# Products with kv in tiles of 32, and a second half laid out anew, in a Hedgehog attention and Mish layer

## The chip, the cores and the metric

The kernel runs on one core of a Trainium2 chip. The metric is the device time of one execution in microseconds; the median of three runs before the change is 182.94 us.

## The reference

```python
def _A_ref(x, wqkv, w_phi, wo):              # H = 32 heads of Dh = 16, S = 2048, D = 512
    q, k, v = qkv[0], qkv[1], qkv[2]         # of x @ wqkv, by heads
    pq = jnp.einsum("bhsd,hdf->bhsf", q, w_phi)
    pk = jnp.einsum("bhsd,hdf->bhsf", k, w_phi)
    phi_q = concatenate([softmax(pq), softmax(-pq)], axis=-1)
    phi_k = concatenate([softmax(pk), softmax(-pk)], axis=-1)
    kv = jnp.einsum("bhsf,bhsd->bhfd", phi_k, v)
    z  = jnp.einsum("bhsf->bhf", phi_k)
    num = jnp.einsum("bhqf,bhfd->bhqd", phi_q, kv)
    den = jnp.einsum("bhqf,bhf->bhq", phi_q, z)[..., None] + 1e-6
    return (num / den by heads side by side) @ wo

def _B_ref(x, w1, b1, w2):                   # F = 1792
    h = x @ w1 + b1
    return (h * tanh(softplus(h))) @ w2

xn = layernorm(x)
return x + _A_ref(xn, wqkv, w_phi, wo) + _B_ref(xn, w1, b1, w2)
```

All inputs and the output are bf16; x is 2048 x 512.

## The kernel before

The 2048 rows are 16 tiles of 128, in four groups of four. Everything is issued in an order written out by hand; each engine works through its own instructions in that order, so what stands early in the text stands early on every engine.

**First half** (the loop over `s` from 0 to 3, lines 505 to 542). Per group: `ln_stats` and `ln_apply` normalise two groups ahead; `value` projects v into `vext`; `logits` projects the keys (folded with w_phi) into `p_sb`; `extremes` (VectorE) subtracts each head's maximum and minimum, over all four tiles at once; `exponentials` (ScalarE) takes the exponentials in place; `normalise` (VectorE) divides by the sums; `accumulate` adds the group's phi_k times v to `pkv` in PSUM. `hidden(n)` computes n units of the first dense layer (each four products of 512 columns) with Mish on ScalarE; they fill TensorE between the steps of the attention.

**Second half** (from line 545). `mask_kv` copies the diagonal blocks of the accumulated kv to `kvm`. Passes 4 to 7 are the queries: `logits`, `extremes`, `exponentials`, which here also issues (through `turn`) DMA transposes of the exponentials into `qT`. `attend(h, i)` multiplies one tile's `qT` with `kvm` into the PSUM tile `pnd`, and ScalarE copies numerators and denominators out of it (lines 350 to 357). `combine(h)` (VectorE) weighs the two planes of two tiles and adds them, and issues a DMA transpose into `ob`. `second_layer(t)` is 14 products of 512 columns into a bank `po`; `project_out(h)` adds four products with `wo` to each of the banks of tiles 2h and 2h+1, and `residual` (VectorE, line 431) adds x and issues the store on SyncE. A bank `po` is held from second_layer(t) to the residual of tile t.

The lines that the prediction uses: in `accumulate` (L285) a product takes 64 columns of the exponentials against 65 of v and ones; two of them, for `r` = 0 and 1, lie side by side in the array by `tile_position=(0, 64 * r)`. In `attend` (L341) a product takes all 128 rows of `qT` against 144 columns of `kvm`, in which the blocks of other heads are zero.

PSUM has eight banks: five in the pool `ps` (all projections, hidden units and `po`), three in `ps2` (`pwide`, then `pkv`, then `pnd`, one at a time).

Of the kernel before, what the change touches and what calls it, by code (L numbers as in the profile page):

```python
# [1 line left out]

# [15 lines left out]
def kernel(  # L18
# [13 lines left out]
    P = 128  # L32
# [26 lines left out]
    ps = ctx.enter_context(tc.tile_pool(name="ps", bufs=5, space=bass.MemoryType.PSUM))  # L59
    ps2 = ctx.enter_context(tc.tile_pool(name="ps2", bufs=1, space=bass.MemoryType.PSUM))  # L60
# [4 lines left out]
    kvm = persist.tile([P, 2, 4, 144], BF16, name="kvm")  # L65
# [14 lines left out]
    KVmask = consts.tile([P, 136], FP32, name="KVmask")  # L80
    vext = [vpool.tile([P, TPG, 4, 2, 68], BF16, name=f"vext{i}") for i in range(2)]
# [11 lines left out]
    def fold(wT, dst, dve):  # L93

        for kt in range(KT):
            pf = ps.tile([P, 512], FP32, name="pfold", tag="mm")
# [40 lines left out]
    def ln_turn_pe(t, xn, i, copy):  # L137
        ptr = ps.tile([P, 512], BF16, name="ptr", tag="mm")
# [12 lines left out]
    def project(w, t, pp=None):  # L151

        if pp is None:
            pp = ps.tile([P, 512], FP32, name="pproj", tag="mm")[:]
# [7 lines left out]
    def value(t, copy):  # L162
        pv = project(wv, t)
        copy(
            vext[(t // TPG) % 2][:, t % TPG, :, :, 0:64].rearrange("p j r c -> p (j r) c"),
            pv.rearrange("p (j c) -> p j c", j=8),
# [4 lines left out]
    def hidden(n):  # L171

        for _ in range(n):
            g, f = next(units)
            ph = ps.tile([P, 512], FP32, name="ph", tag="mm")
# [15 lines left out]
    def logits(s, i, copy):  # L191
        if i == 0:
            p_of[s] = smx.tile([P, TPG, 512], BF16, name="p_sb", bufs=1)
# [3 lines left out]
    def extremes(s, between=None):  # L197

        e = epool.tile([P, TPG, 2, 512], BF16, name="e")
        e_of[s] = e  # L200
        pv = p_of.pop(s)[:].rearrange("p t (c e) -> p (t c) e", e=16)
        for pl, op in enumerate((ALU.max, ALU.min)):
            if pl == 1 and between is not None:
                between()
            src = pv
            for half in (8, 4, 2):
                m = smx.tile([P, 128, half], BF16, name=f"m{half}", bufs=1)
                nc.vector.tensor_tensor(  # L208
                    out=m[:], in0=src[:, :, 0:half], in1=src[:, :, half : 2 * half], op=op
                )  # L210
                src = m[:]

            m = smx.tile([P, 128, 1, 2], BF16, name="m1", bufs=1)
            nc.vector.tensor_tensor(out=m[:, :, 0, :], in0=src, in1=src[:, :, ::-1], op=op)
            mb = m[:].rearrange("p (t c) u o -> p t c u o", t=TPG).to_broadcast(
                [P, TPG, 32, 8, 2]
            )
            p5 = pv.rearrange("p (t c) (e o) -> p t c e o", t=TPG, o=2)
            nc.vector.tensor_tensor(  # L219
                out=e[:, :, pl, :].rearrange("p t (c e o) -> p t c e o", e=8, o=2),  # L220
                in0=p5 if pl == 0 else mb,
                in1=mb if pl == 0 else p5,
                op=ALU.subtract,
            )
# [39 lines left out]
    def blocks(kv, pl, j, width):  # L264

        bank, at = (pl, j) if j < 3 else (2, pl)
        return kv[:, bank, at * 144 : at * 144 + width]

    def by_parts(kv, c0, c1):

        v = kv[:, :, 0:432].rearrange("p b (k c) -> p b k c", c=144)
        return v[:, 0:2, :, c0:c1], v[:, 2, 0:2, c0:c1]

    kv_of = {}

    def accumulate(g):
        if g == 0:
            kv_of[0] = ps2.tile([P, 3, 512], FP32, name="pkv", tag="kv")
        e = e_of.pop(g)
        for j in range(4):  # L280
            for pl in range(2):
                for i in range(TPG):
                    for r in range(2):
                        c = j * P + 64 * r
                        nc.tensor.matmul(  # L285
                            blocks(kv_of[0], pl, j, 65)[64 * r : 64 * r + 64],
                            lhsT=e[:, i, pl, c : c + 64],
                            rhs=vext[g % 2][:, i, j, r, 0:65],
                            start=(g == 0 and i == 0 and (j == 0 or (j == 3 and pl == 0))),
                            stop=(g == NG - 1 and i == TPG - 1),  # L290
                            skip_group_check=True,
                            tile_position=(0, 64 * r),
                        )

    def mask_kv():
        for r in range(2):
            rows, c = slice(64 * r, 64 * r + 64), slice(64 * r, 64 * r + 64)
            a, b = by_parts(kv_of[0], 0, 64)
            nc.vector.tensor_tensor(
                out=kvm[rows, :, 0:3, c], in0=a[rows],  # L300
                in1=KVmask[rows, None, None, c].to_broadcast([64, 2, 3, 64]), op=ALU.mult,
            )
            nc.vector.tensor_tensor(
                out=kvm[rows, :, 3, c], in0=b[rows],
                in1=KVmask[rows, None, c].to_broadcast([64, 2, 64]), op=ALU.mult,
            )
        a, b = by_parts(kv_of[0], 64, 65)
        for pl in range(2):
            nc.vector.scalar_tensor_tensor(
# [311 lines left out]
```

## Time and profile before

| | |
|---|---|
| median of 3 runs | 182.94 us (182.93 to 183.0) |
| the profiled execution | 182.85 us |
| its span on the core | 181.1 us (1.75 us lie around it) |
| TensorE clock granted | 0.999 |
| TensorE busy, VectorE busy, ScalarE busy | 173.9, 146.3, 126.2 us |

Busy times are unions of an engine's instructions. A matmul's duration in the records holds its way through the array, so the records of neighbours overlap; what a product costs is the distance from its start to the next one's start. PE stands for TensorE's products and PEld for its weight loads, DVE for VectorE, ACT for ScalarE, POOL for GpSimdE, SP for SyncE, and a q behind a name for the engine's sequencer. In rows of the chain of work stand start, duration, engine, tile and line; in rows of a timeline also the shapes and in brackets the idle time before, and what ended it. In rows of groups stand the count, the busy time, the mean of one in ns, and the idle time before. In rows of waits stand the total in us, the count and the longest.

### The profile page before, as it was taken

The numbers are of one execution on the slowest core, as the hardware profiler recorded it, in microseconds if no ns is written. First come the engines' busy times: TensorE is split into PE (matmuls) and PEld (weight loads), VectorE is DVE, ScalarE is ACT, GpSimd is POOL, SyncE is SP. The second block draws the span as 40 slices with busy tenths as digits, with TensorE's granted clock in tenths as the row PEclk, the third lists the DMA queues.
The fourth block names the chain that finished last, engine by engine and source line by source line (L and its number), as shares of the span: only waits on it lengthen the run. The fifth ranks groups of instructions, "written<-read, shape, count | busy, mean of one in ns | idle before, by whom it ended". The sixth has DMA issues, their size and how long they took to land.

```text
span 181.1 us, 3005 instructions
## 1 busy us (share of the span) xinstructions
PE 173.9 (96%) x1152; PEld 87.0 (48%) x1167; DVE 146.3 (81%) x254; ACT 126.2 (70%) x194; POOL 26.8 (15%) x34
## 2 busy tenths in 40 slices
PE   6899999999999999998999999999999999999992
PEld 2454344454444545543454545455554545455561
DVE  1989979997999989988999895399917997637963
ACT  2367999999998899969986989472942567235200
POOL 4404069400797000000000000000000000000000
PEclk9999999999999999999999999999999999999999
DMA  6998896300023900000000791953089302990533
GB/s 146 294 390 279 158 346 179 70 1 5 0 58 63 114 0 0 4 0 0 4 0 0 148 87 23 188 136 63 0 177 207 79 5 47 200 192 26 86 91 116
DMA packets 44394, 18.04 MB, mean 100 GB/s; under 512 B 36828, under 2 KB 43868, under 8 KB 44380
## 3 DMA queue, kind: packets, MB, share of 16 engines
q1 hardware_dynamic: 43408, 17.50, 42.8%
q10 hardware_dynamic: 972, 0.35, 0.7%
q8 instruction: 9, 0.15, 0.4%
q14 instruction: 5, 0.04, 0.1%
HBM read 6.84 MB, written 2.10 MB: 49 GB/s over the span
## 4 chain that ended last, share of the span: by engine, by line
PE 50%; DVE 38%; ACT 4%; DMA 4%; issue 2%; POOL 0%; DVEq 0%; POOLq 0%
PE po L414 20%; PE ph L177 8%; DVE s L247 7%; PE po L423 7%; DVE m L208 7%; DVE e L219 5%; PE pproj L156 5%; DVE e L260 4%; ACT e L229 4%; PE pnd L341 3%; DVE r L255 3%; PE warm L463 3%; DVE stats L116 3%; DMA xnT<-xn 2%; DMA ob<-ob 2%
## 5 line engine op out<-in xcount | busy, mean ns | idle before, releaser
L414 PE MATMUL po<-w_sb,acts 128*128 128x512 bf16 (+1 forms) x232 | 50.3, 366 | 0.3
L177 PE MATMUL ph<-xnT,w_sb 128*128 128x512 bf16 x224 | 49.5, 379 | 0.1
L184 ACT ACTIVATE acts<-ph,b1f 128x512 bf16<-128x512 f32 x56 | 35.1, 703 | 2.5 <-PE ph L177 2.3
L177 PEld LDWEIGHTS <-w_sb 128*128 128x128 bf16 x224 | 21.9, 98 | 26.6 <-issue 0.5
L229 ACT ACTIVATE e<-e 128x2048 bf16<-128x2048 bf16 x16 | 29.8, 1903 | 6.9 <-DVE e L219 6.9
L414 PEld LDWEIGHTS <-acts 128*128 128x128 bf16 x238 | 22.8, 98 | 22.0
L156 PEld LDWEIGHTS <-xnT 128*128 128x128 bf16 x192 | 18.2, 98 | 23.0 <-DMA xnT<-xn 1.1
L247 DVE TENSOR_REDUCE s<-e 128x128 f32<-128x2048 bf16 x8 | 18.2, 2277 | 2.6 <-ACT e L229 2.6
L195 ACT CAST p_sb<-pproj 128x512 bf16<-128x512 f32 x25 | 13.7, 587 | 9.4 <-PE pproj L156 9.4
L431 DVE TENSOR_TENSOR x_sb<-po,x_sb 128x512 bf16<-128x512 f32 (+1 forms) x17 | 10.6, 654 | 11.4 <-PE po L423 11.4
L128 POOL TENSOR_SCALAR xn<-x_sb,mv,rstd 128x512 bf16<-128x512 bf16 x8 | 16.7, 2101 | 0.2
L156 PE MATMUL pproj<-wv,xnT 128*128 128x512 bf16 x61 | 15.0, 379 | 0.9 <-ACT p_sb L195 0.8
L423 PE MATMUL po<-wqk,ob 128*128 128x512 bf16 (+1 forms) x66 | 14.7, 366 | 0.3 <-DMA ob<-ob 0.2
L156 PE MATMUL pproj<-wqk,xnT 128*128 128x512 bf16 x62 | 14.4, 379 | 0.1
L350 ACT CAST wkp<-pnd 128x768 bf16<-128x768 f32 x8 | 6.4, 799 | 11.2 <-PE pnd L341 7.3
L116 DVE BATCH_NORM_STATS2 stats<-x_sb 128x6 f32<-128x512 bf16 x16 | 10.0, 679 | 3.8 <-DMA x_sb<-in_A_x_dram 3.8
L208 DVE TENSOR_TENSOR m<-m 128x512 bf16<-128x512 bf16 (+1 forms) x32 | 11.6, 363 | 1.1
L156 PE MATMUL pproj<-wkp,xnT 128*128 128x512 bf16 x50 | 11.8, 379 | 0.1
L208 DVE TENSOR_TENSOR m<-p_sb 128x1024 bf16<-128x1024 bf16 x16 | 11.0, 684 | 0.7 <-ACT p_sb L195 0.7
L341 PEld LDWEIGHTS <-qT 128*128 128x128 bf16 x128 | 9.1, 98 | 3.9 <-issue 0.3
L341 PE MATMUL pnd<-kvm,qT 128*128 128x144 bf16 x128 | 10.6, 226 | 0.0
L350 ACT CAST wv<-pnd 128x768 bf16<-128x768 f32 x8 | 6.3, 792 | 5.9 <-PE pnd L341 3.7
(68 smaller groups left out, 174.8 us busy)
## 6 DMA issues: line engine op xcount, KB each, us to landing
w_sb<-in_B_w_dram SPq DMA_DIRECT2D x2, 1792.0 KB, 9.1
out_dram<-x_sb SPq DMA_DIRECT2D x15, 128.0 KB, 1.8
x_sb<-in_A_x_dram SPq DMA_DIRECT2D x1, 1024.0 KB, 11.8
x_sb<-in_A_x_dram SPq DMA_DIRECT2D x1, 512.0 KB, 4.1
wv<-in_A_wqkv_dram SPq DMA_DIRECT2D x1, 512.0 KB, 4.9
wqk<-in_A_wo_dram SPq DMA_DIRECT2D x1, 512.0 KB
x_sb<-in_A_x_dram SPq DMA_DIRECT2D x1, 256.0 KB, 2.9
x_sb<-in_A_x_dram ACTq DMA_DIRECT2D x1, 256.0 KB, 3.5
```

What stands on the lines that cost most here:

```text
L116: nc.vector.bn_stats(stats[:, i, :], x_sb[:, t0 + i, :])
L128: engine.tensor_scalar(out=xn[:, at + i, :], in0=x_sb[:, t0 + i, :], scalar1=mv[:, i, 0:1], scalar2=rstd[:, i : i + 1], op0=ALU.subtract, ...
L156: nc.tensor.matmul(pp, lhsT=xnT[:, t, kt, :], rhs=w[:, kt, :], start=(kt == 0), stop=(kt == KT - 1),)
L177: nc.tensor.matmul(ph[:], lhsT=w1_sb[:, kt, f * P : (f + 1) * P], rhs=xnT[:, g * TPG : (g + 1) * TPG, kt, :], start=(kt == 0), stop=(kt == ...
L184: nc.scalar.activation(acts[:, f, g * 512 : (g + 1) * 512], ph[:], ACT.Mish, bias=b1f[:, f : f + 1])
L195: copy(p_of[s][:, i, :], pp)
L208: nc.vector.tensor_tensor(out=m[:], in0=src[:, :, 0:half], in1=src[:, :, half : 2 * half], op=op)
L229: nc.scalar.activation(v, v, ACT.Exp)
L247: nc.vector.reduce_sum(t[:], v.rearrange("p t l (c e) -> p (t l c) e", e=16), axis=AX.X)
L341: nc.tensor.matmul(blocks(pnd, pl, j, 144), lhsT=qT_of[h][:, i, pl * 4 + j, :], rhs=kvm[:, pl, j, :], start=True, stop=True,)
L414: nc.tensor.matmul(po[:, c], lhsT=acts[:, f, t * P : (t + 1) * P], rhs=w2_sb[:, f, c], start=(f == 0), stop=False,)
L423: nc.tensor.matmul(po[:, c], lhsT=oT_of[h][:, t % 2 * 4 + j, :], rhs=wo_sb[:, j, c], start=False, stop=(j == 3),)
```

## The change

- `accumulate` uses four tiles of 32 columns side by side, each against 33 columns of v and ones: 128 products per group in place of 64. All of `pkv` lies in one bank, and `vext` has groups of 36 columns in place of 68.
- `attend` uses four tiles of 32 rows, each against 36 columns of `kvm`, into four banks: 32 products in place of 8. ScalarE copies `pnd` out with two instructions in place of four.
- `mask_kv` has two instructions in place of seven, `masks` twelve small copies in place of three and a memset.
- PSUM pools are opened and closed along the way: up to the end of the unit loop of `s` = 0, five banks for projections as before; then seven (`ps`, `px`, `pz`) beside one for `pkv`; in the second half four (`ps`) beside four for `pnd`; in the end one more for the second half of the last tile.
- `extremes` of passes 5 to 7 work in halves of two tiles, `combine` of 0, 2, 3, 4 and 7 tile by tile, and their order around `project_out` is written out anew; the loop over `h` is gone. Two products of second_layer(1) come before attend(0, 0). Pass 7 has its own tile `p_last` for the logits.
- `residual` no longer issues the store; `store()` issues those that wait, later in the order.

```diff
     def accumulate(g, pk):
...
-                    for r in range(2):
-                        c = j * P + 64 * r
+                    for r in range(4):
+                        c = j * P + 32 * r
                         nc.tensor.matmul(
-                            blocks(kv_of[0], pl, j, 65)[64 * r : 64 * r + 64],
-                            lhsT=e[:, i, pl, c : c + 64],
-                            rhs=vext[g % 2][:, i, j, r, 0:65],
+                            kv_of[0][32 * r : 32 * r + 32, pl, j, :],
+                            lhsT=e[:, i, pl, c : c + 32],
+                            rhs=vext[g % 2][:, i, j, r, 0:33],
...
-                            tile_position=(0, 64 * r),
+                            tile_position=(0, 32 * r),
...
-        pnd = ps2.tile([P, 3, 512], FP32, name="pnd", tag="kv")
+        pnd = later[0].tile([P, 4, 512], FP32, name="pnd", tag="nd")
         for pl in range(2):
             for j in range(4):
-                nc.tensor.matmul(
-                    blocks(pnd, pl, j, 144),
-                    lhsT=qT_of[h][:, i, pl * 4 + j, :],
-                    rhs=kvm[:, pl, j, :],
+                for r in range(4):
+                    at, rows = (pl * 4 + j) * 36, slice(32 * r, 32 * r + 32)
+                    nc.tensor.matmul(
+                        pnd[:, r, at : at + 36],
+                        lhsT=qT_of[h][rows, i, pl * 4 + j, :],
+                        rhs=kvm[rows, pl, j, :],
...
+                        tile_position=(32 * r, 0),
...
+        a = pnd[:, :, 0:288].rearrange("p r (l j c) -> p l j r c", l=2, j=4)
+        to = nm[:, i, :, :].rearrange("p l (j r c) -> p l j r c", j=4, r=4)
+        nc.scalar.copy(to, a[:, :, :, :, 0:32])
+        nc.scalar.copy(ds[:, i], a[:, :, :, :, 32:36])
...
     def residual(t, po, c, queue):
         y = x_sb[:, t, c]
         nc.vector.tensor_tensor(out=y, in0=po[:, c], in1=y, op=ALU.add)
-        queue.dma_start(o_v[:, t, c], y)
+        waiting.append((queue, o_v[:, t, c], y))
...
+            hidden(6)
+            turns[0] = cycle([pz, ps, ps, pz, ps, px, ps])
+        hidden((5, 14, 8, 10)[s])
         extremes(s + 1)
...
     second_layer(0)
     hidden(2)
+    second_layer(1, 0, 2)
     attend(0, 0)
-    second_layer(1, 0, 8)
+    second_layer(1, 2, 12)
     attend(0, 1)
-    extremes(5)
-    second_layer(1, 8)
-    combine(0)
-    exponentials(5)
+    extremes(5, halves=low)
+    second_layer(1, 12)
+    combine(0, first)
+    combine(0, last)
+    extremes(5, halves=high)
+    exponentials(5, (0,))
     second_layer(2)
     attend(1, 0)
     second_layer(3)
     attend(1, 1)
...
+    project_out(0)
+    combine(1)
+    store()
+    for i in range(TPG):
+        logits(6, i, act)
+    attend(2, 0)
+    exponentials(5, (1,))
+    second_layer(4)
+    extremes(6, halves=low)
+    attend(2, 1)
+    exponentials(6, (0,))
+    second_layer(5)
+    combine(2, first)
+    project_out(1)
+    combine(2, last)
+    store()
+    attend(3, 0)
+    second_layer(6)
+    combine(3, first)
+    attend(3, 1)
+    second_layer(7)
+    combine(3, last)
+    project_out(2)
+    store()
+    for i in range(TPG):
+        logits(7, i, act)
+    extremes(6, halves=high)
+    attend(4, 0)
+    exponentials(6, (1,))
+    second_layer(8)
+    extremes(7, halves=low)
+    attend(4, 1)
+    exponentials(7, (0,))
+    second_layer(9)
+    combine(4, first)
+    project_out(3)
+    combine(4, last)
+    store()
+    attend(5, 0)
+    second_layer(10)
+    extremes(7, halves=high)
+    attend(5, 1)
+    exponentials(7, (1,))
+    second_layer(11)
+    project_out(4)
+    combine(5)
+    store()
+    attend(6, 0)
+    second_layer(12)
+    attend(6, 1)
+    second_layer(13)
+    combine(6)
+    attend(7, 0)
+    project_out(5)
+    combine(7, first)
+    attend(7, 1)
+    combine(7, last)
+    store()
+    after.close()
+    later.append(ctx.enter_context(tc.tile_pool(name="pe", bufs=1, space=PSUM)))
+    second_layer(14)
+    second_layer(15)
+    project_out(6)
+    store()
+    project_out(7)
+    store()
```

More of the change, by code (lines that the diff above doesn't have):

```diff
@@ L79 @@
     block = consts.tile([P, 8, 16], BF16, name="block")
-    KVmask = consts.tile([P, 136], FP32, name="KVmask")
-    vext = [vpool.tile([P, TPG, 4, 2, 68], BF16, name=f"vext{i}") for i in range(2)]
+    KVmask = consts.tile([P, 34], FP32, name="KVmask")
+    vext = [vpool.tile([P, TPG, 4, 4, 36], BF16, name=f"vext{i}") for i in range(2)]
     ctx.enter_context(tc.manual_schedule())
@@ L95, in fold @@
         for kt in range(KT):
[L96 removed]
+            pf = bank("pfold")
             for j in range(4):
@@ L153, in project @@
         if pp is None:
-            pp = ps.tile([P, 512], FP32, name="pproj", tag="mm")[:]
+            pp = bank("pproj")[:]
         for kt in range(KT):
@@ L410, in second_layer @@
         if f0 == 0:
-            po_of[t] = [ps.tile([P, 512], FP32, name="po", tag="mm") for _ in halves(t)]
+            po_of[t] = [
+                bank("po", FP32, later[1] if c.stop == 512 and c.start else None)
+                for c in halves(t)
+            ]
         for po, c in zip(po_of[t], halves(t)):
```

232 lines of the change are left out of this document (106 added, 126 removed).

## The prediction

> **What bounds the kernel now.** I read the page first, then the chain of work that ended last, then the timelines of TensorE, ScalarE, VectorE and SyncE in the second half.
>
> ```profile
> PE 173.9 (96%) x1152; PEld 87.0 (48%) x1167; DVE 146.3 (81%) x254; ACT 126.2 (70%) x194; POOL 26.8 (15%) x34
> ...
> PE 50%; DVE 38%; ACT 4%; DMA 4%; issue 2%; POOL 0%; DVEq 0%; POOLq 0%
> ```
>
> TensorE is busy for 96% of the span, yet only half of the chain is TensorE; over a third is VectorE. Both are nearly full, and where the chain changes hands tells which one a saving must come from:
>
> ```profile
> 42.72 0.69 DVE vext L164
> ...
> 111.53 3.18 DMA ob<-ob
> ...
> 114.76 1.90 PE po L423 x8
> ...
> 123.63 0.50 PE pnd L341 x8
> 124.13 3.02 PE po L414 x14
> 127.15 1.73 PE po L423 x8
> ```
>
> From 42.72 to 111.53 the chain runs mainly through VectorE (normalise, extremes, combine(0)), then through one DMA transpose into project_out(0) at 114.76, and from there through TensorE alone. Three prices come from these rows: an attend is 0.50 us on TensorE, a second_layer 3.02, a project_out 1.73 (0.865 per tile). Three waits matter:
>
> ```profile
> 41.86 0.69 DVE L164 CAST vext<-pproj 128x512 bf16<-128x512 f32 x1 [1.38 <-PE pproj L156]
> ...
> PE pproj L156 <- ACT p_sb L195: 0.8, 1, 0.8
> ...
> PE po L423 <- DMA ob<-ob: 0.2, 1, 0.2
> ```
>
> At 41.86 VectorE waits for TensorE, so what accumulate(0) saves moves the VectorE chain. After that VectorE sets the pace up to combine(0): time that accumulate(1) to (3) save, or the 0.8 us wait for a bank that the seven banks may remove, lets TensorE reach attend(0,0) sooner, but not its transposed input. The 0.2 is the wait at 114.76.
>
> **The products with kv.** Today one accumulate, with its neighbours:
>
> ```profile
> 38.69 1.03 PE L177 MATMUL ph<-xnT,w_sb 128*128 128x512 bf16 x4
> 39.65 1.20 PE L285 MATMUL pkv<-vext,e 128*64 128x65 bf16 x64
> 40.79 0.39 PE L156 MATMUL pproj<-wv,xnT 128*128 128x512 bf16 x1
> L285 PE MATMUL pkv<-vext,e 128*64 128x65 bf16 x256 | 4.8, 196 | 0.0
> ```
>
> A product of 512 columns takes 3.02/14 = 0.216 us, so the last of the four before starts at 38.69 + 3 x 0.216 = 39.34 and streams until 39.56. The 64 products then begin within 1.20 - 0.196 = 1.0 us, and the next full one starts at 40.79. The block costs 1.23: 32 pairs at 31.5 ns, and 0.23 for going into the tiled form and out of it again.
>
> The price of columns: 0.50/8 = 62.5 ns for 144 and 216 for 512 give 0.417 ns per column and 2.4 fixed, so 29.5 ns for 65. The measured pair, 31.5, is just above that: the two tiles of a pair run side by side. Four tiles would take, per set of four, between 17.4 ns (36 columns, all four side by side, the same for 33 within 1.2 ns) and 31.5 (what two tiles take now, with as many columns in all). I take the middle, 24.5. [...]
>
> An accumulate becomes 32 sets: 0.23 + 32 x 0.0245 = 1.01, saving 0.22. An attend becomes 8 sets, and now it too changes the tiling, which it didn't before: 0.23 + 8 x 0.0245 = 0.43, saving only 0.07 of 0.50 each, 16 x 0.075 = 1.2 us. Most of what smaller products give goes back into 32 more changes of form. With 17.4 and 31.5 an attend is 0.37 or 0.48. The trace has no row tiles: if changing to them cost nothing, an attend would be 0.14 (third rival), and if loads don't overlap it would be above 0.5 (first rival).
>
> **Around attend(0,0).**
>
> ```profile
> 103.18 0.66 PE L341 MATMUL pnd<-kvm,qT 128*128 128x144 bf16 x8
> ...
> 99.50 5.38 SPq L238 DMA_TRANSPOSE qT<-e  x4
> ...
> DMA to landing us min/median/max: 3.2/3.3/4.8
> ...
> 97.45 0.54 DVE L299 TENSOR_TENSOR kvm<-pkv,KVmask 64x384 bf16<-64x384 f32 x1
> ...
> 99.25 1.88 DVE L195 CAST p_sb<-pproj 128x512 bf16<-128x512 f32 x3
> ```
>
> Its input, the first transpose of qT, lands at 99.50 + 3.3 = 102.8 and TensorE comes at 103.18. After: the VectorE chain is 0.2 earlier (accumulate(0)), so the input is there at 102.6. TensorE has two more products of second_layer(1) ahead of it (0.43), and is earlier by 4 x 0.22 + 0.8 = 1.7: it would come at 101.9 and waits until 102.6. So of the first half's 1.7 us there remain 0.58, and the 0.43 already done: 1.0 us. On VectorE mask_kv falls from seven steps in 1.8 us (97.45 to 99.25) to two, about 0.5 by the nearest rows, and the first half of extremes(5) no longer waits for the fourth cast. That makes room for combine(0) in halves; with it the transposes of combine(0) come before TensorE asks for them, and the wait ahead of 114.76 (0.2 us) goes.
>
> **ScalarE.** One eviction:
>
> ```profile
> 104.22 0.80 ACT L350 CAST wkp<-pnd 128x768 bf16<-128x768 f32 x1
> ...
> 105.29 0.23 ACT L357 COPY ds<-pnd 128x32 f32<-128x32 f32 x1
> ```
>
> Four copies take 1.30 us from 104.22 to 105.52. Two copies of 1024 and 128 elements, at the slope of these rows, take some 1.16. ScalarE has room in the second half, so I put it at nothing; if runs of 32 elements out of four banks cost 0.4 us more, the next attend waits 0.4 once, at (0,1), since elsewhere 3.02 us of second_layer lie between.
>
> **VectorE, and four banks in place of five.**
>
> ```profile
> 101.78 0.69 DVE L208 TENSOR_TENSOR m<-p_sb 128x1024 bf16<-128x1024 bf16 x1 [0.65 <-ACT p_sb L195]
> ...
> 107.74 0.28 DVE L373 TENSOR_TENSOR u<-ds 128x128 f32<-128x128 f32 x1
> ...
> 115.83 0.69 DVE L431 TENSOR_TENSOR x_sb<-po,x_sb 128x512 bf16<-128x512 f32 x1 [4.33 <-PE po L423]
> ...
> 117.30 0.28 DVE L373 TENSOR_TENSOR u<-ds 128x128 f32<-128x128 f32 x1
> ...
> 120.99 0.68 DVE L208 TENSOR_TENSOR m<-p_sb 128x1024 bf16<-128x1024 bf16 x1
> ...
> 167.74 0.22 DVE L373 TENSOR_TENSOR u<-ds 128x64 f32<-128x64 f32 x1
> ...
> 170.25 1.28 DVE L431 TENSOR_TENSOR x_sb<-po,x_sb 128x512 bf16<-128x512 f32 x2
> L208 DVE TENSOR_TENSOR m<-m 128x512 bf16<-128x512 bf16 x16 | 6.8, 428 | 0.6
> L208 DVE TENSOR_TENSOR m<-m 128x256 bf16<-128x256 bf16 x16 | 4.8, 299 | 0.5
> L391 DVE TENSOR_TENSOR wv<-wv,f 128x1024 bf16<-128x1024 bf16 x2 | 1.4, 692 | 0.1
> ```
>
> A whole extremes takes 107.74 - 101.78 = 5.96. A half, for each of max and min, is 0.43 (512 elements), 0.30 (256), 0.235 (128, by the slope of those two), about 0.23 for the last fold, 0.69 for the subtraction, with 0.03 between: 1.9, so 3.8 a half and 1.6 more per pass, 4.9 for three passes. A half combine takes 170.25 - 167.74 = 2.5. A whole one took about 3.7 (117.30 to 120.99) and gets two more small steps, 4.05 (0.22 each in place of half of a 0.28). Five combines in halves in place of one, and three whole ones: some 6 us more. So VectorE gets about 11 us more work in the second half, where it has waits like the 4.33 us above. Two places have no cover for it:
>
> Before project_out(2), VectorE does residual(3), which ends 0.9 us after project_out(1) (0.21 for the result to arrive, 0.69), then three half combines, 7.5: residual(4) ends 8.4 + 0.7 = 9.1 us after project_out(1). TensorE does two attends, two second_layers and project_out(2) in 0.86 + 6.04 + 1.73 = 8.6 and then wants a bank for logits(7): of four, two hold tiles 6 and 7, the others wait for residuals 4 and 5. New wait: 0.4.
>
> Before project_out(5), VectorE does residual(9) (0.9 after project_out(4)), combine(5) 4.05, and the transposes land 3.2 later: 8.1. TensorE has three attends and two second_layers, 7.3. New wait: 0.8.
>
> SyncE issues 13 transposes of ob in place of 9, at 5.38/4 = 1.35 us each at most, and the stores behind them; its waits are long, and a store that goes later delays nobody but at the end, where the order of the last residuals and stores is as before. Nothing for that.
>
> **The sum**, against the profiled execution (span 181.1, 1.75 us around it, 182.85; the median is 182.94): -1.0 (to attend(0,0)) - 1.2 (attends) - 0.2 (wait at 114.76) + 0.4 + 0.8 = -1.2. With 17.4 ns per set -1.9, with 31.5 -0.7. I forecast 181.6, with 180.9 to 182.2 as this case's own range.
>
> **The rivals.** *Loads and products don't come closer than now.* 64 loads and products took 1.0 us, 15.7 ns for each. If a row tile's load and product keep that pace, an attend is 0.23 + 32 x 0.0157 = 0.73, slower by 0.23: 16 x 0.23 = +3.7, the two new waits vanish behind longer attends, -1.0 - 0.2 + 3.7 = +2.5, 185.3. It decides above 0.0105 us per load and product. For it:
>
> ```profile
> L341 PEld LDWEIGHTS <-qT 128*128 128x128 bf16 x128 | 9.1, 98 | 3.9 <-issue 0.3
> L482 PEld LDWEIGHTS <-b1b 14*128 14x128 bf16 x1 | 0.1, 90 | 0.1
> ```
>
> A load of 14 rows takes 90 ns where 128 rows take 98, and there are four times as many. Against it: the pitch inside accumulate is that of the columns, so nothing shows a limit on loads. [...] If accumulates keep that pace too (128 x 0.0157 + 0.23 = 2.2, +1.0 each, four of them, less the bank wait), it is about 189. Chance 0.24, of which 0.06 for the latter.
>
> *VectorE becomes the bound.* If each half piece costs 0.25 more than worked out, the wait at logits(7) grows by three pieces, 0.75, a like one of 0.6 opens at logits(6), where combine(1) follows two residuals that follow a half extremes, and 0.2 and 0.4 come ahead of project_out(5) and the last one: +2.0, 183.6. It decides at about 0.15 a piece. For it: VectorE is 81% busy and gets 11 us more. Against: the half combine is measured. Chance 0.13.
>
> *Changing to row tiles costs nothing.* Attends of 0.14 save 5.8, but VectorE's lateness gives some 3.9 back in all (1.2 worked out above, the rest at the same places by the same 0.3 us per attend): -1.0 - 5.8 - 0.2 + 3.9 = -3.1, 179.8. Against it, the 0.23 of accumulate. Chance 0.13.
>
> **The numbers.** The forecast has 0.50. A measurement of this kernel can tell about 0.2% (0.37 us) from no change. Faster: 0.13 and nearly all of the forecast, 0.44: 0.57. Same: 0.06. Slower: 0.24 + 0.13 = 0.37. The range 180.0 to 185.5 leaves out half of the third rival, the accumulate part of the first and a little of its upper side: under 0.2.
>
> **What would show it.** In the changed profile: 8 sets of four in an attend within 0.37 to 0.48 us from the end of one 512-column product to the next; an accumulate near 1.0; TensorE waiting some 0.7 us for qT ahead of attend(0,0), 0.4 for VectorE ahead of logits(7), 0.8 for ob ahead of project_out(5). An attend above 0.55, or waits of TensorE for residuals of 1 us and more, would make the forecast wrong.

## The result and the profile after

The changed kernel takes 182.28 us (median of 6 runs, 181.76 to 182.54) against 182.94 (6 runs, 182.78 to 183.24): a ratio of 0.9957 with a 95% interval of 0.9939 to 0.9976, 0.66 us or 0.4% less. Faster was forecast, by 1.3 us; the time is inside the range, and 0.1 above the forecast case's own one. The profiled execution is the fastest of the six: 181.76 us, span 179.8, clock 0.997.

From the page of the changed kernel: busy times with counts, the instruction fetches of TensorE (queue q8), and the shares of the chain. Lines have moved: attend's products stand at L337, accumulate's at L290, second_layer at L415, project_out at L424, the residual at L432.

```profile
PE 170.8 (95%) x1785; PEld 81.8 (46%) x1807; DVE 154.0 (86%) x313; ACT 123.9 (69%) x162; POOL 29.6 (16%) x42
q8 instruction: 14, 0.23, 0.5%
DVE 47%; PE 33%; ACT 8%; DMA 8%; issue 2%; DVEq 0%; ACTq 0%; SPq 0%
```

TensorE's loads and products rose by about half, from 2319 to 3592, and with them the fetches, from 9 to 14; before, that row read:

```profile
q8 instruction: 9, 0.15, 0.4%
```

TensorE's timeline after, at the places the prediction named:

```profile
39.41 1.20 PE L290 MATMUL pkv<-vext,e 128*32 128x33 bf16 x128
40.54 1.90 PE L168 MATMUL pproj<-wv,xnT 128*128 128x512 bf16 x7
...
102.44 0.37 PE L337 MATMUL pnd<-kvm,qT 32*128 32x36 bf16 x32 [0.15 <-DMA qT<-e]
...
112.40 0.37 PE L337 MATMUL pnd<-kvm,qT 32*128 32x36 bf16 x32
112.70 1.04 PE L424 MATMUL po<-wqk,ob 128*128 128x512 bf16 x4
114.35 1.04 PE L424 MATMUL po<-wqk,ob 128*128 128x512 bf16 x4 [0.61 <-DMA ob<-ob]
115.22 3.69 PE L168 MATMUL pproj<-wqk,xnT 128*128 128x512 bf16 x15
...
134.21 1.89 PE L424 MATMUL po<-wqk,ob 128*128 128x512 bf16 x8
136.26 3.61 PE L168 MATMUL pproj<-wqk,xnT 128*128 128x512 bf16 x16 [0.15 <-DVE x_sb L432]
139.80 0.37 PE L337 MATMUL pnd<-kvm,qT 32*128 32x36 bf16 x32
140.11 3.20 PE L415 MATMUL po<-w_sb,acts 128*128 128x512 bf16 x13
143.24 0.37 PE L337 MATMUL pnd<-kvm,qT 32*128 32x36 bf16 x32
143.54 3.20 PE L415 MATMUL po<-w_sb,acts 128*128 128x512 bf16 x13
...
163.86 0.37 PE L337 MATMUL pnd<-kvm,qT 32*128 32x36 bf16 x32
164.82 1.90 PE L424 MATMUL po<-wqk,ob 128*128 128x512 bf16 x8 [0.59 <-DMA ob<-ob]
```

Read starts against starts, since a wait in brackets begins only at the modelled end of the product before, some 0.16 us past its pitch: a product of 512 columns is recorded with 379 ns, and the next one starts 216 ns after it. One attend with one second_layer takes 143.54 - 140.11 = 3.43, where it took 3.52. Of that the attend has 0.40: 0.30 from its start to the next product (139.80 to 140.11) and 0.10 from the end of the full products before it. project_out(0) takes 115.22 - 112.70 = 2.52 for eight products worth 1.73: 0.79 is lost there. logits(7) comes 2.05 after project_out(2) began: 0.32 lost. From 163.86, 0.96 to project_out(5) in place of 0.30: 0.66 lost.

Against the profiled execution before, in span (all from these rows and those of before; negative is gained):

| step | forecast | this execution | the second one, below |
|---|---|---|---|
| to attend(0,0), from 103.18, with the 0.43 of second_layer(1) done before it | -1.0 | -1.17 | -0.99 |
| 16 attends at 0.09 | -1.2 | -1.4 | -1.4 |
| wait for ob(0), where 0.36 was lost before by the same reading | -0.2 | +0.43 | +0.70 |
| wait at logits(7) | +0.4 | +0.32 | +0.31 |
| wait at project_out(5) | +0.8 | +0.66 | +0.61 |
| sum of the span | -1.2 | -1.2 | -0.8 |
| by the spans themselves | | -1.3 | -0.9 |
| time around the span (1.75 before) | 0 | +0.21 | +0.26 |

The 0.36 before is 114.76, where project_out(0) began, less 114.40, where the attend ahead of it (0.50) ended:

```profile
113.90 0.66 PE L341 MATMUL pnd<-kvm,qT 128*128 128x144 bf16 x8
```

So this execution gained 1.09; a usual one gains less, as the second column of measurements has it.

### The profile page after: what moved, and what is told of

It is laid out like the page before. It is cut to its first block, busy times and chain, and to the rows that moved or that the text cites. A ratio compares the mean times of both kernels' runs of the same rounds, so it can differ in the third digit from the quotient of the medians.

```text
span 179.8 us, 4310 instructions
## 1 busy us (share of the span) xinstructions
PE 170.8 (95%) x1785; PEld 81.8 (46%) x1807; DVE 154.0 (86%) x313; ACT 123.9 (69%) x162; POOL 29.6 (16%) x42
## 4 chain that ended last, share of the span: by engine, by line
DVE 47%; PE 33%; ACT 8%; DMA 8%; issue 2%; DVEq 0%; ACTq 0%; SPq 0%
PE po L415 14%; DVE s L262 7%; DVE m L225 6%; PE po L424 6%; PE ph L189 6%; PE pproj L168 5%; ACT e L244 5%; DVE stats L128 5%; DVE e L234 5%; DVE e L275 4%; DMA ob<-ob 4%; DVE r L270 3%; DMA qT<-e 2%; DVE x_sb L432 2%; DMA x_sb<-in_A_x_dram 2%
## 5 line engine op out<-in xcount | busy, mean ns | idle before, releaser
L415 PE MATMUL po<-w_sb,acts 128*128 128x512 bf16 (+1 forms) x224 | 50.2, 366 | 0.8 <-PE pnd L337 0.2
L415 PEld LDWEIGHTS <-acts 128*128 128x128 bf16 x238 | 22.2, 98 | 22.5
L347 ACT CAST wv<-pnd 128x1024 bf16<-128x1024 f32 x8 | 8.1, 1010 | 14.5 <-PE pnd L337 12.3
L424 PE MATMUL po<-wqk,ob 128*128 128x512 bf16 (+1 forms) x67 | 15.1, 367 | 1.3 <-DMA ob<-ob 1.2
L432 DVE TENSOR_TENSOR x_sb<-po,x_sb 128x512 bf16<-128x512 f32 (+1 forms) x17 | 11.0, 658 | 5.7 <-PE po L424 5.7
L209 ACT CAST p_sb<-pproj 128x512 bf16<-128x512 f32 x21 | 11.3, 587 | 4.9 <-PE pproj L168 4.9
L225 DVE TENSOR_TENSOR m<-m 128x256 bf16<-128x256 bf16 (+2 forms) x44 | 13.4, 305 | 1.5
L347 ACT CAST wkp<-pnd 128x1024 bf16<-128x1024 f32 x8 | 8.1, 1014 | 3.5 <-PE pnd L337 3.4
L275 DVE TENSOR_TENSOR e<-e,r 128x2048 bf16<-128x2048 bf16 x8 | 10.3, 1282 | 0.3
L424 PEld LDWEIGHTS <-ob 128*128 128x128 bf16 x68 | 6.4, 98 | 8.3 <-DMA ob<-ob 1.8
L225 DVE TENSOR_TENSOR m<-p_sb 128x1024 bf16<-128x1024 bf16 (+1 forms) x18 | 10.2, 565 | 0.0
```

Of the source, the lines that this page charges most:

```text
L225: nc.vector.tensor_tensor(out=m, in0=src[:, :, 0:half], in1=src[:, :, half : 2 * half], op=op)
L275: nc.vector.tensor_tensor(out=vv, in0=vv, in1=r2[:, :, None, :].to_broadcast([P, 128, 8, 2]), op=ALU.mult)
L347: nc.scalar.copy(to, a[:, :, :, :, 0:32])
L415: nc.tensor.matmul(po[:, c], lhsT=acts[:, f, t * P : (t + 1) * P], rhs=w2_sb[:, f, c], start=(f == 0), stop=False,)
L424: nc.tensor.matmul(po[:, c], lhsT=oT_of[h][:, t % 2 * 4 + j, :], rhs=wo_sb[:, j, c], start=False, stop=(j == 3),)
```

## Experiments

**The changed kernel once more**, unedited, to see what is the same in every execution.

> The changed kernel, not edited. Its six runs lie between 181.76 and 182.54 us, wider apart than those of before. Theory: its chain passes several times through DMA transposes of ob that nothing covers, and their landing varies (2.4 to 4.7 us in one profile), so a second profile that is 0.4 us longer shows it in the waits of TensorE for ob. Rival: it varies at the start (loads of x and of the weights), so the difference is there before 40 us. About 182.2 in either case.

Measured: 182.30 us (181.94 to 182.56), ratio 0.9969 (0.9957 to 0.9981); the profiled one 182.21, span 180.2. Its timeline at the same places, and the chain's pieces for the transposes that it waits for:

```profile
102.62 0.37 PE L337 MATMUL pnd<-kvm,qT 32*128 32x36 bf16 x32
...
112.62 0.37 PE L337 MATMUL pnd<-kvm,qT 32*128 32x36 bf16 x32
112.93 1.04 PE L424 MATMUL po<-wqk,ob 128*128 128x512 bf16 x4
114.85 1.04 PE L424 MATMUL po<-wqk,ob 128*128 128x512 bf16 x4 [0.89 <-DMA ob<-ob]
115.72 1.53 PE L168 MATMUL pproj<-wqk,xnT 128*128 128x512 bf16 x6
...
134.71 1.89 PE L424 MATMUL po<-wqk,ob 128*128 128x512 bf16 x8
136.75 1.46 PE L168 MATMUL pproj<-wqk,xnT 128*128 128x512 bf16 x6 [0.15 <-DVE x_sb L432]
...
164.35 0.37 PE L337 MATMUL pnd<-kvm,qT 32*128 32x36 bf16 x32
165.26 1.90 PE L424 MATMUL po<-wqk,ob 128*128 128x512 bf16 x8 [0.53 <-DMA ob<-ob]
```

```profile
110.33 4.47 DMA ob<-ob
162.19 3.02 DMA ob<-ob
```

Of the difference of 0.45 to the first profile, 0.18 is there at attend(0,0) (102.62 for 102.44; accumulate(0) began at 39.63 for 39.41, after a slower start of the kernel), and 0.27 comes from project_out(0): 2.79 for eight products worth 1.73, 1.06 lost. Its transposes take 4.47 us from issue to use, those of ob(5) 3.02. The whole change gains 0.66; this one wait costs more than that. The time around the span, too, differs: it is 1.96 to 2.04 in all 11 runs of the changed kernel and 1.66 to 1.76 in the runs of the kernel before: 0.28 us, outside everything that the trace shows.

**The two halves of the change apart.** First the order alone: the changed kernel with the products with kv as they were (two tiles of 64 in accumulate, eight full products in attend, three banks for `pkv`, so without the seven banks of the first half; `pnd` keeps its four banks and fills three).

```diff
-        pk.tile([P, 2, 4, 33], ...)
+        pk.tile([P, 3, 512], ...)
...
-                    for r in range(4):
-                        c = j * P + 32 * r
+                    for r in range(2):
+                        c = j * P + 64 * r
...
-                for r in range(4):
-                    nc.tensor.matmul(pnd[:, r, at : at + 36], ..., tile_position=(32 * r, 0))
+                nc.tensor.matmul(blocks(pnd, pl, j, 144), ...)
```

> The order, the halves and the four banks of the change, with the products of before: accumulate in two tiles of 64, attend in 8 whole products, four evictions, seven steps of mask_kv. Theory that the tiles carry the gain: an attend costs 0.50 us again where the changed kernel shows 0.40, 16 x 0.10 = 1.6 us, of which the waits at logits(7) and project_out(5) swallow some 0.5: 1.0 us slower than the changed kernel, 183.0 to 183.5, no faster than before. Rival that the order carries it: within 0.3 us of the changed kernel, about 182.3.

Measured: 184.06 us (183.99 to 184.31), ratio 1.0071 (1.0058 to 1.0084): slower than the kernel before by 1.2, which is more than was expected. Its waits of TensorE:

```profile
PE po L432 <- DVE p_sb L209: 1.4, 1, 1.4
...
PE pproj L168 <- ACT p_sb L209: 0.8, 1, 0.8
```

The 0.8 is the bank wait of before, back again. The 1.4 was not expected: the casts that free the banks of logits stand in VectorE's order behind mask_kv, which here has its seven instructions (97.35 to 99.16 us) where the changed kernel's two take 0.41. attend(0,0) starts at 105.07, 2.6 us later than in the changed kernel. So the new order by itself costs 1.2; with the short mask_kv and the banks that one-bank kv frees, these two waits of 1.4 and 0.8 are not there. Which of the two frees TensorE from the 1.4, no run tells.

Then the tiles alone: four tiles of 32 everywhere and four banks beside four, with the order of before in the second half (whole extremes and combines, stores at once).

```diff
+    for h in range(2 * NG):
+        t = 2 * h + 4
...
+        if h in (1, 3, 4, 5):
+            combine(h + 1)
...
+        project_out(h)
+        if h in (0, 2):
+            combine(h + 1)
```

> The products in tiles of 32 and the four banks, with the order of before: whole extremes and combines, stores with the residuals. Theory that four banks need the new order: in the profile of before the residuals follow combine(2), (4) and (6) and come some 2 us after their products; with four banks second_layer(6), (10) and (14) wait for them, 2 to 2.5 us each, less 1.6 for the attends: 186 to 189 us. Rival that the order matters little: 181.5.

Measured: 194.17 us (192.72 to 195.12, the four runs whose granted clock was 0.98 or more; two at 0.974 took 197.2 and 197.31), ratio 1.0614 (1.0577 to 1.065), well above the 186 to 189 expected. The waits of TensorE, project_out(0) in its timeline, its transposes in the chain, and the instruction fetches of TensorE from 114 to 116.5 us:

```profile
PE po L415 <- DVE x_sb L432: 8.4, 4, 2.7
PE po L424 <- DMA ob<-ob: 2.5, 1, 2.5
```

```profile
116.57 3.39 PE L424 MATMUL po<-wqk,ob 128*128 128x512 bf16 x8 [2.50 <-DMA ob<-ob]
```

```profile
111.76 4.76 DMA ob<-ob
```

```profile
q8 instruction: 1, 0.02, 3.0%
```

Three of the four waits for residuals came where they were worked out, 2.5 to 2.7 each; the fourth, 0.59 ahead of second_layer(12), was not foreseen. The 2.5 at project_out(0) was not expected, nor that it costs twice: its eight products then took 3.39 us in place of 1.9. Most of it is not the order's doing: a fetch began at 114.40 us, while these transposes were under way, and they took 4.76 us where the next two of ob in this run took 3.0 and 3.1 (the second theory below shows why). The waits for residuals stay, 8.4 in all, and attends were as short as in the changed kernel. So with four banks the tiles need the new order, as the order needs the tiles; as they were run here neither half is worth anything alone, and only together they gain 0.66.

**Where the expected gain went: first theory, VectorE is late.** The last two hidden units, eight products, move from behind second_layer(0) into the first half, so that their Mish on ScalarE no longer stands ahead of the first eviction.

```diff
-        hidden((5, 14, 8, 10)[s])
+        hidden((5, 14, 8, 12)[s])
...
-    hidden(2)
```

> The changed kernel with its last two hidden units moved from behind second_layer(0) to the end of the first half (12 in place of 10). ScalarE then has no table load and no two Mish between the exponentials of pass 4 and the first eviction (2.55 us), and the eviction of attend(0,0) can begin at about 102.6 in place of 103.9. Theory that VectorE's idle 1.9 us ahead of combine(0) makes project_out(0) wait 0.6 us for its second tile: that wait goes, 0.5 us faster than the changed kernel. Rival that the transpose's landing (4.2 us there) is what is late whatever VectorE does: no more than 0.2 us faster.

Measured: 181.61 us (180.96 to 181.92), ratio 0.9928 (0.991 to 0.9946). Faster, and the theory falls all the same: combine(0)'s transposes were issued 0.8 us sooner (107.08 for 107.88) and the wait was still there.

```profile
114.62 1.04 PE L424 MATMUL po<-wqk,ob 128*128 128x512 bf16 x4 [0.64 <-DMA ob<-ob]
```

```profile
109.60 4.97 DMA ob<-ob
```

The transposes took still longer. So VectorE is not what holds them. (The profiled execution, 181.92, is the longest of this kernel's six; what the shorter ones did otherwise is not shown.)

**Second theory: an instruction fetch falls on the transposes.** The DMA view of the window from 112 to 114.5 us, in the second run of the changed kernel: the rate in 40 slices of 0.06 us, the transposes' queue, and one 16 KB fetch.

```profile
GB/s 205 193 217 38 9 0 0 0 0 262 0 0 4 82 180 233 213 209 209 193 225 176 168 111 41 20 0 0 0 0 8 4 8 8 12 8 8 12 8 8
q1 hardware_dynamic: 686, 0.17, 89.5%
q8 instruction: 1, 0.02, 3.2%
```

686 small packets kept 16 DMA engines busy for 89.5% of 2.5 us: 52 ns each in the mean. The mean hides two kinds. In the trace's packet records 668 of them took 20 ns; the other 18 began between 113.32 and 113.60 us and took 1.10 to 1.38 us, ending together by 114.73. So the transposes stood still for over a microsecond, as the end of the rate's row shows; the fetch is recorded from 112.62 to 113.92. To take the fetch from there without touching the order, eight of the warm products at the start were cut into 64 shorter ones of as many columns in all; TensorE's program is then 112 instructions longer at its head, so the fetches come sooner.

```diff
-    for _ in range(12):
+    for _ in range(4):
...
+    for _ in range(64):
+        nc.tensor.matmul(warm[:, 0:64], lhsT=ident[:], rhs=ident[:, 0:64], ...)
```

> The changed kernel, with 8 of the 12 warming products of 512 columns cut into 64 of 64 columns: as much work, but 112 instructions more at the start of TensorE's stream, so that each later fetch of 16 KB of instructions comes 112 instructions earlier. In three profiles of the changed order a fetch at 112.5 us falls on the transposes of ob(0) and qT(2): their packets of 256 bytes then take over 1 us in place of 0.02, the second transpose of ob(0) lands after 4.2 to 5.0 us in place of 2.5, and project_out(0) waits 0.6 to 0.9. Theory that the fetch causes it: it moves to about 109.2, that wait goes, and the wait for ob(5) ahead of project_out(5) stays or grows by up to 1 us, as a fetch comes to 163.9 there; the time is within 0.7 us of the changed kernel on either side. Rival that the transposes of qT(2) behind it cause it: the wait stays at 0.6 to 0.9.

Measured: 181.22 us (181.14 to 181.25), ratio 0.9905 (0.9888 to 0.9921). The same views, the timeline first:

```profile
112.64 0.37 PE L337 MATMUL pnd<-kvm,qT 32*128 32x36 bf16 x32
112.94 1.90 PE L424 MATMUL po<-wqk,ob 128*128 128x512 bf16 x8
114.78 3.61 PE L168 MATMUL pproj<-wqk,xnT 128*128 128x512 bf16 x16
```

```profile
q1 hardware_dynamic: 1369, 0.33, 70.2%
```

attend(1,1) starts within 0.02 us of where it did and the transposes were issued at 107.89 for 107.88, so nothing ahead differs; the fetch now falls at 106.95 us, where no transposes are under way. Twice the packets pass, at 70.2% of 16 x 2.5 us / 1369 = 21 ns each, none above 0.1 us, and project_out(0) has no wait: it takes 1.84 (112.94 to 114.78) in place of 2.79. These 0.95 us are nearly all of the 0.98 by which the two profiled executions differ (181.23 for 182.21; the medians, 1.08). Moving the fetch moved the wait: this is shown.

The packet records of all fourteen profiles bear it out. They have 70 pauses in which five or more packets of at most 512 bytes took over 0.5 us each. Of these, 68 begin between 0.13 us before and 1.10 us after the recorded start of a TensorE fetch, and all 68 end 0.67 to 0.91 us after its recorded end. Of the 174 transposes of ob, 35 had a fetch begin after their issue and at least 0.8 us before their landing: they took 2.83 to 4.97 us, 4.16 in the median; the other 139 took 2.40 to 3.39, 2.44 in the median.

*Placing a fetch on another transpose.* The counter-test: 106 short products, and then 100, to bring a fetch onto ob(5)'s transposes.

```diff
+    for _ in range(106):
+        nc.tensor.matmul(warm[:, 0:39], ...)
```

> The shifted kernel with 106 short warming products in place of 64 (39 columns each, the same columns in all): 84 instructions more. [...] Theory that a fetch holds up the transposes beside it: the wait for ob ahead of project_out(5) grows from 0.57 to 1.3 to 2 us, 0.7 to 1.3 us slower than the shifted kernel, 181.9 to 182.5. Rival that the shift helped by something else (the warm-up, the start): no wait grows, 181.0 to 181.4.

Measured: 181.15 us (181.05 to 181.49), ratio 0.9903 (0.9889 to 0.9918). The fetch came at 160.91 us and was over at 162.05, before the packets of ob(5) flowed, from about 162.2; the wait at project_out(5) stayed at 0.54. With 100:

> The shifted kernel with 100 short warming products (41 columns each): 72 instructions more than with 64, 12 fewer than with 106. With 106 the fetch came at 160.9 to 162.05 us, ahead of the packets of ob(5), whose issue ends at 162.4, and no wait grew. Here it should come at 162.5 to 163, on those packets. Theory that a fetch holds up the transposes beside it: the wait ahead of project_out(5) grows from 0.55 to between 1.2 and 2 us, 0.6 to 1.3 us slower than the shifted kernel: 181.8 to 182.4. Rival that the fetch has no part in it: 0.55 us and 181.2.

Measured: 181.31 us (181.22 to 181.58), ratio 0.9917 (0.9903 to 0.993); fetch at 160.85, wait 0.53. Both missed their target, so a wait for ob(5) was not made. With 106 another fetch, at 113.92, did meet transposes, those of qT(2): they took 4.6 and 4.1 us where they took 3.2 in the kernel with 64 short products, but TensorE did not need them yet, and no wait followed. A fetch on the transposes is not enough; they must also be the next thing that TensorE wants. And the gain does not hang on one length: three lengths of the program's head, each with the fetch away from ob(0), lie within 0.2 us.

**Why accumulates gained almost nothing.** Theory, named after a queue that no record shows: TensorE is fed only so fast with loads and products, so that fewer columns leave the block as long as it is; rival: the columns of the products set the pitch. The probe halves the columns, leaving out half of v, so its results are not the layer's; only its time is read.

```diff
-                            kv_of[0][32 * r : 32 * r + 32, pl, j, :],
+                            kv_of[0][32 * r : 32 * r + 32, pl, j, 0:17],
...
-                            rhs=vext[g % 2][:, i, j, r, 0:33],
+                            rhs=vext[g % 2][:, i, j, r, 16:33],
```

> A probe: the changed kernel, whose accumulate takes 17 moving columns in place of 33 (half of v and the ones; the numerators of every second head are then wrong heads' values). Loads and the number of products stay. In the changed kernel the 128 products start over 1.01 us, as long as the 64 of before: the first 8 sets of four 25 ns apart, the rest 33 ns. [...] Rival that the columns set the pace (132 in a set of four, 130 in a pair of before): 0.55 us, at most 0.8 with a floor of 25 ns.

Measured: 182.0 us (one run). Its timeline, beside which stand the changed kernel's 39.41 and 40.54 above:

```profile
39.75 1.18 PE L290 MATMUL pkv<-vext,e 128*32 128x17 bf16 x128
40.86 0.82 PE L168 MATMUL pproj<-wv,xnT 128*128 128x512 bf16 x3
```

1.11 against 1.13: half the columns save 0.02, so columns do not set it. They don't set the pace of the first eight sets either: in both kernels' records the first 32 products start within 0.20 us, 25 ns for a set of four. The other probe issues each attend's products twice:

```diff
-        for pl in range(2):
+        for pl in (0, 1, 0, 1):
```

> A probe: the changed kernel with the products of every attend issued twice (same results), 64 in place of 32. Theory of the queue: the first 32 start within 0.20 us as now, 6.3 ns apart, the other 32 come 8.3 ns apart: 0.47 us from first to last start. Rival that four row tiles are simply quicker than four column tiles: all 64 at 6.3 ns, 0.40 us. What is left of an attend, 0.2 us for the two changes of form, is the same in both.

Measured: 185.19 us (one run). One attend in its timeline, and its products begun up to 141.70 us beside all of them (durations in ns, then first and last start):

```profile
141.49 0.66 PE L337 MATMUL pnd<-kvm,qT 32*128 32x36 bf16 x64
142.08 3.19 PE L415 MATMUL po<-w_sb,acts 128*128 128x512 bf16 x14
```

```profile
L337 PE MATMUL pnd<-kvm,qT x33: 172/173/188, 141.5 to 141.7; 32*128 32x36 bf16 x33
L337 PE MATMUL pnd<-kvm,qT x64: 172/180/188, 141.5 to 142.0; 32*128 32x36 bf16 x64
```

33 products begin in the first 0.21 us, 6.3 ns apart, the other 31 in the next 0.27, 8.6 ns apart (the last starts at 141.49 + 0.66 - 0.18 = 141.97). The attend takes 0.59 in place of 0.30. The same break stands in accumulate, in the changed kernel: 31 of its 128 begin up to 39.61 us, 0.20 after the first, the other 97 in the 0.81 that follow, 8.3 ns apart. The paces of the theory hold: some 32 loads and 32 products go at the tiles' pace, 6.3 ns a product, and after those a load with its product takes 8.3 to 8.6 ns, with 17, 33 and 36 columns alike. So an attend, 32 loads and 32 products, is through before the break, and an accumulate, 128 of each, has three quarters of its products behind it. Whether the loads or the feeding of TensorE set those 8.3 ns is not separated: each product here has a load of its own. That a queue makes the break is the author's conjecture; the runs show where it is, not what makes it.

**What is better than both.** Combines were shortened: the weights' multiplication writes them doubled and in bf16 (no cast after it), with the denominators laid out by ScalarE in two copies so that it reads them in order.

```diff
-        nc.scalar.copy(ds[:, i], a[:, :, :, :, 32:36])
+        for x in range(2):
+            nc.scalar.copy(ds[:, i, :, x]..., a[:, :, :, :, 32 + 2 * x : 34 + 2 * x])
...
                 nc.vector.tensor_tensor(
-                    out=uh[:, i], in0=ds[:, k, ::-1, 1], in1=wh[:, i], op=ALU.mult
+                    out=f[:, k],
+                    in0=ds[:, k, ::-1, 1, :, None].to_broadcast([P, 2, 32, 2]),
+                    in1=w[:, k, None, :, None].to_broadcast([P, 2, 32, 2]),
+                    op=ALU.mult,
                 )
-            nc.vector.tensor_copy(f[:, q]..., u[:, q]...)
```

By itself:

> The changed kernel with the weights of combine written out doubled by the multiplication, hidden units where they were. With hidden units moved too it was 180.36, 1.25 us less than with them moved alone, where 0.3 to 0.5 were expected. Theory that most of that came from the second transpose of ob(0) landing ahead of the fetch at 112: here combine(0) still waits for ScalarE's two Mish, its transpose goes out at about 109.9 as in the changed kernel less 0.4, and meets the fetch: 181.7 to 182.0, wait ahead of project_out(0) 0.3 or more. Rival that VectorE's shorter combines are worth 1.2 us by themselves: 181.0.

Measured: 180.72 us (180.5 to 181.16), ratio 0.988 (0.9862 to 0.9897), 1 us better than expected. A half combine is shorter by 0.19 (105.89 to 108.16, 2.27, for 2.46); the rest is the fetch: in this kernel it fell at 113.15, when ob(0) had landed.

```profile
113.20 0.37 PE L337 MATMUL pnd<-kvm,qT 32*128 32x36 bf16 x32
113.51 1.90 PE L418 MATMUL po<-wqk,ob 128*128 128x512 bf16 x8
```

Against the kernel with the moved fetch (181.22), which has no such wait either, the shorter combines are worth 0.5 by the medians. The profiled execution, 181.16, is this kernel's longest and came to attend(1,1) 0.56 late (113.20 for 112.64); both spans are 179.2, so from there on it is 0.56 shorter, 0.19 of it at ob(5)'s wait (0.38 for 0.57) and 0.15 at logits(7), where there is none. Together with the earlier hidden products:

> The kernel with the hidden units moved, and with the weights of combine written out doubled and in bf16 by the multiplication itself, in place of a multiplication and a cast; the denominators are copied out of PSUM by two ScalarE instructions, x apart, in place of one. VectorE's half combine should fall from 2.46 to about 2.27 us, a whole one from 3.83 to 3.6; ScalarE's eviction grows by 0.13. Theory that VectorE is what TensorE waits for at logits(7) (0.15) and, through ob(5), at project_out(5) (0.55): both shrink by 0.2 to 0.4, 0.3 to 0.5 us faster than with the hidden units moved alone, 181.1 to 181.3. Rival that these waits are the transposes' landing: no more than 0.1 us.

Measured: 180.36 us (180.3 to 180.57), ratio 0.9861 (0.9846 to 0.9875), 0.7 below the lowest expected: the fetch came at 111.98, when ob(0) had landed (111.71), so the wait at project_out(0) went too. Its one wait for ob:

```profile
163.56 1.90 PE L418 MATMUL po<-wqk,ob 128*128 128x512 bf16 x8 [0.29 <-DMA ob<-ob]
```

And all three edits:

> Hidden units moved, weights written out by the multiplication, and the instructions shifted by 112. Theory: the wait ahead of project_out(0) is gone already, so the shift can only move a fetch on or off ob(5), of which 0.29 us of wait are left: within 0.4 us of 180.36. Rival that the shift gives 1.1 us here as it did in the changed kernel: 179.3.

Measured: 180.32 us (180.25 to 180.64), ratio 0.9861 (0.9844 to 0.9877). The moved fetch adds nothing where the transposes land ahead of it anyway. This and the one before it are the best versions that were run, the same within their spread: 2.6 us below the kernel before, 2.0 below the changed one.

## Why the prediction came out as it did

The direction was right, and so was the largest term; half of the size is missing. By the steps of the prediction:

- *Attends*, the largest term: right, and a little better: 0.40 for a forecast 0.43. Eight sets of four at 25 ns and about 0.2 for the change of form both hold, for row tiles as for column tiles. That 24.5 was so near is luck, though: it was the middle between two prices of columns, and a set takes 25 ns with 17 columns as with 33 and 36. The first rival (15.7 ns for each load and product) is out for attends, but the thought behind it, a limit on loads and products and not on columns, is what rules accumulates: 8.3 ns for a load with its product, and 0.02 us saved with half the columns.
- *Accumulates*: the step "32 sets x 24.5 ns" failed. They take 1.19 and save 0.04, not 0.22: from 39.35, where the full products before end (28.96 and 48 of 0.2165), to 40.54. One pitch, worked out from columns, was taken for an attend of 64 instructions and an accumulate of 256 alike, and past some 64 a load with its product takes 8.3 ns, with 17 columns as with 33. It cost little in the end, since only VectorE's start at accumulate(0) hung on it.
- *To attend(0,0)*: 102.62 in the second execution, for a forecast 102.6 (the first began accumulate(0) 0.2 sooner and was at 102.44). The bank wait of 0.8 is gone, as worked out. But TensorE was to come at 101.9 and wait some 0.7 for qT. It was through with the two products ahead at 102.12 and 102.34 and waited some 0.2, beside 0.1 for the change of form: accumulates had not brought it there so much sooner. The start came right because the landing of qT set it, at 102.39 and 102.58. That accumulate(0)'s saving would move VectorE's chain as well was wrong, and changed little.
- *The wait for ob(0)*: the step that failed, in its sign. It was to go, since the transposes of combine(0) come before TensorE asks for them; it cost 0.79 in one profile and 1.06 in the other, for 0.36 before. The issue was early enough: the second tile's transposes went out at 110.11, and with the 3.27 us that they took in the kernel with the moved fetch would have landed at 113.38, while TensorE wanted them at 113.57. What the prediction did not count is TensorE's own instructions: 64 more products in each of 4 accumulates and 24 in each of 16 attends, each with its load, are 1280 more, which q8's row shows as five more fetches; one of them met these transposes, and they stood still.
- *logits(7) and project_out(5)*: 0.32 and 0.66 for 0.4 and 0.8. Half extremes took 3.8 as worked out, a half combine 2.46 for 2.5, a whole combine 3.82 for 4.05.
- *ScalarE*: "some 1.16" for an eviction; measured 1.18 (103.87 to 105.05).
- *Around the span*: taken as unchanged at 1.75; it is 2.00 in the mean. The order alone has 1.73, the tiles alone 2.12, so it comes with the tiles. It is not the count of TensorE's instructions: twice the products in attend left it at 1.99. What it is stays open.
- *The second rival*, VectorE as the bound, asked for waits that grow by 0.25 a piece; they did not. *The third*, no cost for changing the form, asked for an attend of 0.14.

So of the 1.3 us forecast some 0.9 went to ob(0)'s transposes (+0.70 where -0.2 was worked out) and 0.3 around the span; attends and the two smaller waits gave 0.5 back. For the second execution the terms make -0.8 and +0.26, the measured medians -0.6.

What stays open: why the earlier hidden products alone gained 0.7 although their profile keeps the wait, what lies in the 0.28 around the span, and by what way a fetch stops the transposes' packets.

## What to carry to other kernels

Small tiles side by side paid in short bursts: an attend of 32 loads and 32 products fell from 0.50 to 0.40 us, of which some 0.2 are for going into the tiled form and out of it again; a long run of them goes at 8.3 ns a pair after the first 64 instructions, and there half the columns gained 0.02 us of 1.13. More instructions were also more fetches, 14 in place of 9: compare the instruction queue's row before and after, and when a wait for a DMA transpose grows though it was issued no later, look whether a fetch stands in its window. A few instructions more at the head of the program tell, and cost nothing here: with 112 more the time was 181.22 us in place of 182.30.

## What the runs showed of the hardware

- Four tiles of 32 side by side start 25 ns apart by sets, for the first eight sets of a burst; after those 64 instructions, a 32-wide load with its product takes 8.3 to 8.6 ns. Both hold for 17 columns as for 33 (128 products and the change of form in 1.11 and 1.13 us), and for row tiles of 36 columns (6.3 and 8.6 ns a product) as for column tiles.
- One 16 KB fetch of TensorE's instructions stopped DMA transposes of many small packets: 18 packets took 1.10 to 1.38 us where 20 ns are usual, the flow went on 0.67 to 0.91 us after the fetch's end in all 68 such pauses on record, and the second transpose of ob(0) took 4.1 to 5.0 us in the four profiles where a fetch met it, and 3.3 with the fetch moved. No wait of TensorE is put down to a fetch itself; by way of the transposes one cost 0.95 us.
- In the kernel with the tiles alone, TensorE's granted clock fell from 1.00 to 0.55 after a wait of 2.5 us. In its windows the granted clock stands behind the busy times:

```profile
114.00:116.00 2.00, 0.07 (x12) 0.00 (x0) 0.00 (x0) 1.18 (x2) 0.00 (x0) 1.00 1.33 98
116.00:118.00 2.00, 1.43 (x4) 0.58 (x5) 0.00 (x0) 0.00 (x0) 0.00 (x0) 0.55 0.96 194
118.00:120.00 2.00, 2.00 (x7) 0.70 (x5) 0.69 (x1) 0.00 (x0) 0.00 (x0) 0.59 0.98 189
120.00:122.00 2.00, 2.00 (x10) 0.87 (x9) 1.90 (x7) 0.78 (x2) 0.00 (x0) 1.00 0.76 205
```

It was 0.55 to 0.59 for some 4 us, which cost 1.5 us more (3.39 - 1.9). Three later waits of 2.5 to 2.7 us in that kernel were followed by products at full pace, so the length of the wait alone does not decide. Over its six runs the time goes with the mean granted clock, from 192.72 us at 0.999 to 197.31 at 0.974.
